# A recurrent kernel's small transfers issued by GpSimd instead of ACT and SP, with a ring of five pieces and 20 of 64 streamed

## The chip, the cores and the metric

The kernel runs on one core of one Trainium2 chip. Its time is device microseconds from start to end of the program on that core; lower is better. All weights and inputs lie in HBM, and the output goes there.

## What is computed

The output is `g * a + (1 - g) * b` for 2048 rows of 1024 numbers, all in bf16. `b` is a feed-forward layer: `gelu(x @ w_gate) * (x @ w_up) @ w_down` with 3584 columns inside. `a` is an attention layer with a memory, which runs over 64 segments of 32 rows one after the other:

```python
g = sigmoid((x * gate_w).sum(-1, keepdims=True))
mem = mem0                                   # 8 rows of 1024
for s in range(64):
    h = concat([mem, x[32*s:32*s+32]])       # 40 rows
    q, k, v = h @ Wq, h @ Wk, h @ Wv         # 32 heads of 128 columns
    p = softmax(masked(q @ k.T * 128**-0.5)) # causal; all rows see the memory
    o = (p @ v) @ Wo                         # 40 rows of 1024
    mem = o[:8]                              # the next segment's memory
    out_a[s] = o[8:]
```

The memory rows make the segments depend on each other: segment s+1 can't start its projections of the memory before segment s has its output rows.

## The kernel before

The program has three stages. A setup (to about 244 us) transposes `x` into a scratch tensor `xq_scr`, computes the gate values, loads the resident weights and computes q, k and v of the last 8 rows of every segment for all segments at once, into the scratch tensors `qk_scr` and `v_scr`. The recurrence (to about 2421 us) runs 64 steps, one for each segment. The last stage is the feed-forward layer, in four blocks of 512 rows, with the mixing of both parts.

**The weights of the recurrence** are Wq, Wk, Wv and Wo, cut into 64 pieces of 128 x 2048 numbers (512 KB, 4 KB in each partition). A step uses the pieces in a fixed order: 8 each of k, q, k, q, v, v (positions 0 to 47), then 16 of Wo (positions 48 to 63). They don't all fit into SBUF: `NRES` of them are resident, and the others are streamed from HBM anew in every step, through a ring of `NRING` buffers. `NRES` is what the memory below the ring leaves: with a ring of 4 it is 45, so 19 of 64 pieces are streamed; the list `streamed` spreads them over the positions by weights. `load_str` (L349) issues the load of the next streamed piece in the order `seq`, on SP's queue, right after the code of the piece that frees a place; the instruction itself waits only for the last readers of its own ring buffer (`ring[n % NRING]`). The setup loads the first pieces, four ahead of their use. A load of 512 KB is one DMA.

**A step** (`for s in range(NSEG)`): `proj(p, s)` is called for the 64 positions in turn, and a table `on(position, function)` puts the rest of the step's work in front of some of them: copies out of PSUM, transposes, scores, softmax, attention. The output is collected in the PSUM bank A0 and copied to `a_bf`; PE transposes it, and DVE copies the 8 memory rows into the `hT` of the next step (L893). That copy closes the step. In this layout a step computes the memory rows and the first 24 rows; the other 8 rows of each segment are collected in `oTR` for four segments, and in every fourth step (s % 4 == 3) Wo is applied to them too: each of its 16 pieces is then used twice, the second time two positions later (`lag`), and the loads that follow on a ring piece are issued after the second use. The result goes to `a_rb`.

**The small transfers of a step**: `load_h` (L488) fetches `hT` of the next step (64 KB) at position 5, `load_qk` (L492) fetches `qkr` (128 KB) at position 33, `load_v` (L496) fetches `vB` (128 KB) for two steps at position 56. `store` (L902, L906) writes `a_bf` (64 KB) into the scratch tensor `a_scr`, and after s % 4 == 3 also `a_rb` in four parts of 16 KB; since these parts overwrite rows that the store of `a_bf` wrote, each waits until that store has landed. `store` is put in a list (`pend`) and issued at position 2 of the next step, behind three of the copies of `put_rest` on POOL. ACT issues `load_h`, `load_qk`, `load_v` and the store of `a_bf`; SP issues the four stores of `a_rb`. The last stage reads `a_scr` long after.

POOL has in a step four copies of `put_rest` (three at position 2, the fourth, `qT` of the second half, at position 30, read by the second `scores` at position 40) and two of `keep_o`.

**Waits.** `_Prog` records every operation with what it reads and writes, and each engine runs its operations in the order of the program, waiting on semaphores for the others. A DMA stands in the queue of the engine that issues it, and its wait holds what is queued behind it. Operations of POOL are chained to each other by a dependency (`self.pool`).

In the text a step is named by its s; "step 0 of each four" is a step with s % 4 == 0.

Of the kernel before, what the change touches and what calls it, by code (L numbers as in the profile page):

```python
# [30 lines left out]
class _Prog:  # L31
# [47 lines left out]
    def op(self, eng, fn, rd=(), wr=(), lane=None, after=()):  # L79
        o = _Op(eng, fn)  # L80
        if lane is not None:
            ln = self.lanes.get(lane)
            if ln is None:
                ln = self.lanes[lane] = [self.new_sem(f"{self.name}_{lane}"), 0, None]
            if ln[2] is not None:
                o.deps.append(ln[2])
            ln[1] += 16
            o.sem, o.val, o.inc, o.need = ln[0], ln[1], 16, True
            ln[2] = o
        for r in rd:  # L90
            self._touch(o, r, False, lane is not None)
        for r in wr:
            self._touch(o, r, True, lane is not None)
        o.deps.extend(after)
        if eng == "pool":
            if self.pool is not None:
                o.deps.append(self.pool)
            self.pool = o
        for d in o.deps:
            d.need = True  # L100
        o.idx = len(self.ops)
        self.ops.append(o)
        return o
# [92 lines left out]
def bass_gated_mix__memory_aug_recurrent_mem_tr__geglu_ffn__prompt_kernel(  # L196
# [16 lines left out]
    S, D = xf.shape  # L213
    _, H, Dh = A_Wq.shape
    M = A_mem0.shape[1]
    SEG = 32
    NR = 24
# [4 lines left out]
    KC = D // 128  # L222
    FF = B_w_gate.shape[1]
    NJ = FF // 128
    NRING = 4
    scale = float(Dh) ** -0.5
    NEG = -1.0e9
    LQ = 40
# [3 lines left out]
    with ExitStack() as es:  # L232
# [10 lines left out]
        xq_scr = nc.dram_tensor("xq_scr", [NT, 128, 4, KC * SEG], BF16)  # L243
        qk_scr = nc.dram_tensor("qk_scr", [128, NSEG, 4, 128], BF16)
        v_scr = nc.dram_tensor("v_scr", [NSEG // 2, 4, 32, 512], BF16)
# [70 lines left out]
        op = P.op  # L316
# [76 lines left out]
        xrT = al("xrT", [128, KC, NRT])  # L393
        stq = [al(f"stq{i}", [128, max(NSEG, 64), 128]) for i in range(2)]
        xq = [al(f"xq{i}", [128, 4, KC, SEG]) for i in range(2)]
        gwb = al("gwb", [128, D])
        assert cur[0] <= top

        tmpv = {p: al(f"tmpv{p}", [128, 2048], at=stq[0].off + PIECE * n) for n, p in enumerate(p for p in str_qkv if p >= 32)}
# [1 line left out]
        vr = [p for p in res if 32 <= p < 48]  # L401
        cur[0] = res[vr[0]].off
        px = [al(f"px{i}", [128, D]) for i in range(min(NT, 16))]
        gp = al("gp", [128, D], FP32, at=xb[0])
        pr = [al(f"pr{i}", [128, D], at=xb[0] + 2048 * i) for i in range(2)]
        memT = al("memT", [128, 64], at=oTR[1].off)
# [78 lines left out]

        def load_h(s):
            t = hT[s % 2]
            op("act", lambda e: e.dma_start(t[:, :, :].rearrange("p k c -> p (k c)"), xq_scr[s // 4, :, s % 4, :]),  # L488
               rd=[("D", "xq", s // 4)], wr=[t.r()], lane=f"h{s % 2}")

        def load_qk(s):
            op("act", lambda e: e.dma_start(qkr[:, :, :], qk_scr[:, s, :, :]), rd=[("D", "qk", m) for m in range(4)],  # L492
               wr=[qkr.r()], lane="qkr")

        def load_v(s):
            op("act", lambda e: e.dma_start(vB[:, :, :].rearrange("p j c -> p (j c)"), v_scr[s // 2].rearrange("g r c -> (g r) c")),  # L496
               rd=[("D", "v", s // SB, g, u) for g in range(4) for u in range(2)], wr=[vB.r()], lane="vb")

        nb2 = [0]
# [336 lines left out]
        for s in range(NSEG):  # L836
# [62 lines left out]
                act_copy(a_rb[:, :], PB[A1][:, 0:256], [BK(A1)], [a_rb.r()])  # L899

            def store(s=s):
                op("act", lambda e: e.dma_start(a_scr[s].rearrange("r (g c) -> g r c", g=4), a_bf[:, :]), rd=[a_bf.r()],  # L902
                   wr=[("D", "a", s)], lane="st")
                if s % 4 == 3:
                    for g in range(4):
                        op("sp", lambda e, g=g: e.dma_start(a_scr[s - 3:s + 1, NR:SEG, 256 * g:256 * g + 256], a_rb[32 * g:32 * g + 32, :]),  # L906
                           rd=[a_rb.r()] + [("D", "a", t) for t in range(s - 3, s + 1)], wr=[("D", "ar", s // 4, g)], lane=f"sr{g}")
            pend.append(store)
        for f in pend:
# [114 lines left out]
```

## Time and profile before

| | |
|---|---|
| median of 3 runs | 3046.32 us (3031.21 to 3049.27) |
| the profiled execution | 3029.77 us, span 3028.0 us |
| busy: PE, DVE, ACT, POOL | 2381.8, 756.8, 627.8, 170.2 us |
| moved by DMA | 805.02 MB |
| mean granted clock of TensorE | 0.930 |

Busy time counts work on the engine; the span is the time from the first to the last instruction. All rows below come from the one profiled execution. In the view of windows, each row has the stretch, its length, the busy time of five engines with instructions in brackets, the granted clock, the mean busy share of the 16 DMA engines and the GB/s that they moved.

### The profile page before, as it was taken

Reading aid. Unit: us, or ns where it says so; the run is one execution under the profiler, and the core shown is the slowest. Engines: PE = TensorE matmul, PEld = TensorE weight load, DVE = VectorE, ACT = ScalarE, POOL = GpSimd, SP = SyncE. Lnnn points to the kernel's source line nnn. Section 1 sums busy time; section 2 is a strip of 40 time slices with the busy share of each in tenths; the row PEclk is TensorE's granted clock in tenths of the full one; section 3 lists DMA queues with packets and bytes.
Section 4 is the critical chain, followed back from the end, with each engine's and each line's share of the span. In section 5 each row is a group of like instructions: output and inputs, shape, how many; then the busy total and the mean of one; then the engine's idle time right before and its main releaser. Section 6 shows DMA issues by size and latency. Waiting matters only on the chain.

```text
span 3028.0 us, 87815 instructions
## 1 busy us (share of the span) xinstructions
PE 2381.8 (79%) x40486; PEld 1104.2 (36%) x40486; DVE 756.8 (25%) x1829; ACT 627.8 (21%) x1461; POOL 170.2 (6%) x487
## 2 busy tenths in 40 slices
PE   7686777777777777777777777777777799999998
PEld 3332333333333333333333333333333344444443
DVE  1311211212121111211121211211121152626262
ACT  1111221222221212212121221222122131313130
POOL 3300000000000000000000000000000000000000
PEclk9798989989999889989898998999899999999999
DMA  8637989989898988989898988989898956060605
GB/s 316 203 120 278 324 294 314 321 297 327 298 330 290 312 296 309 314 290 328 281 323 283 315 305 286 325 299 324 283 324 296 325 213 226 10 229 8 229 8 181
DMA packets 341425, 805.02 MB, mean 266 GB/s; under 512 B 58808, under 2 KB 103864, under 8 KB 341056
## 3 DMA queue, kind: packets, MB, share of 16 engines
q1 hardware_dynamic: 269680, 757.18, 72.3%
q10 hardware_dynamic: 71376, 42.22, 4.6%
q8 instruction: 317, 5.19, 0.7%
q14 instruction: 52, 0.43, 0.0%
HBM read 773.08 MB, written 26.21 MB: 264 GB/s over the span
## 4 chain that ended last, share of the span: by engine, by line
DMA 53%; PE 39%; issue 3%; DVE 2%; SPq 1%; POOL 1%; ACT 1%; ACTq 1%; POOLq 0%
DMA ring<-in_A_Wv_dram 17%; DMA ring<-in_A_Wk_dram 17%; PE pb L941 11%; PE pb L793 10%; DMA ring<-in_A_Wo_dram 7%; DMA ring<-in_A_Wq_dram 7%; PE pb L819 6%; PE pb L978 5%; PE pb L517 2%; DMA a_scr<-a_bf 2%; DMA wd<-in_B_w_down_dram 1%; PE pb L545 1%; POOL gp L475 1%; DMA qk_scr<-stq 1%; PE pb L674 1%
## 5 line engine op out<-in xcount | busy, mean ns | idle before, releaser
L793 PE MATMUL pb<-ring,hT 128*32 128x512 bf16 x3840 | 417.8, 423 | 446.5 <-DMA ring<-in_A_Wk_dram 180.2
L793 PE MATMUL pb<-res,hT 128*32 128x512 bf16 x8448 | 708.7, 417 | 1.1 <-issue 1.1
L793 PEld LDWEIGHTS pb<-ring,hT 128*32 128x32 bf16 x3840 | 106.5, 95 | 623.8 <-DMA ring<-in_A_Wk_dram 215.2
L793 PEld LDWEIGHTS pb<-res,hT 128*32 128x32 bf16 x8448 | 237.4, 102 | 185.4 <-issue 60.0
L657 ACT ACTIVATE tok<-pb 128x512 bf16<-128x512 f32 (+1 forms) x256 | 139.2, 544 | 734.9 <-PE pb L793 729.8
L819 PE MATMUL pb<-res,oT 128*32 128x256 bf16 x6144 | 266.3, 289 | 11.9 <-issue 9.8
L941 PE MATMUL pb<-xT,wg 128*128 128x512 bf16 x896 | 211.8, 379 | 8.4 <-DVE GT L957 8.4
L941 PE MATMUL pb<-xT,wu 128*128 128x512 bf16 x896 | 211.7, 379 | 0.0
L978 PE MATMUL pb<-wd,GT 128*128 128x512 bf16 x896 | 195.5, 379 | 6.7 <-DMA wd<-in_B_w_down_dram 6.7
L819 PEld LDWEIGHTS pb<-res,oT 128*32 128x32 bf16 x6144 | 166.5, 102 | 55.2 <-issue 25.2
L819 PE MATMUL pb<-ring,oT 128*32 128x256 bf16 x2048 | 108.3, 284 | 53.5 <-DMA ring<-in_A_Wo_dram 47.8
L700 DVE TENSOR_REDUCE nm<-pb 128x8 f32<-128x320 f32 x128 | 62.9, 491 | 307.8 <-PE pb L696 307.8
L949 ACT ACTIVATE s<-pb 128x512 f32<-128x512 f32 x112 | 66.8, 596 | 315.1 <-PE pb L941 295.6
L941 PEld LDWEIGHTS pb<-xT,wg 128*128 128x128 bf16 x896 | 86.9, 98 | 116.5 <-DVE GT L957 12.8
L978 PEld LDWEIGHTS pb<-wd,GT 128*128 128x128 bf16 x896 | 87.0, 98 | 114.6 <-DMA wd<-in_B_w_down_dram 11.1
L941 PEld LDWEIGHTS pb<-xT,wu 128*128 128x128 bf16 x896 | 87.7, 98 | 105.7
L517 PE MATMUL pb<-xrT,res 128*128 128x512 bf16 x368 | 101.0, 390 | 29.3 <-DMA ring<-in_A_Wq_dram 29.3
L660 DVE CAST oT<-pb 128x160 bf16<-128x160 f32 x256 | 71.1, 319 | 203.5 <-PE pb L774 203.5
L657 ACT ACTIVATE oT<-pb 128x160 bf16<-128x160 f32 x256 | 63.8, 301 | 270.2 <-PE pb L774 270.2
L660 DVE COPY qT<-pb 128x512 bf16<-128x512 bf16 (+1 forms) x128 | 45.8, 358 | 279.7 <-PE pb L674 187.2
L950 DVE SCALAR_TENSOR_TENSOR tp<-s,pb 128x512 f32<-128x512 f32 x112 | 76.9, 687 | 135.4 <-ACT s L949 135.3
L660 DVE COPY kT<-pb 128x512 bf16<-128x512 bf16 x64 | 27.2, 424 | 329.5 <-PE pb L674 329.5
(101 smaller groups left out, 2278.3 us busy)
## 6 DMA issues: line engine op xcount, KB each, us to landing
ring<-in_A_Wv_dram SPq DMA_DIRECT2D x384, 512.0 KB, 6.2
ring<-in_A_Wq_dram SPq DMA_DIRECT2D x325, 512.0 KB, 6.0
ring<-in_A_Wk_dram SPq DMA_DIRECT2D x260, 512.0 KB, 5.8
ring<-in_A_Wo_dram SPq DMA_DIRECT2D x256, 512.0 KB, 5.8
wd<-in_B_w_down_dram SPq DMA_DIRECT2D x56, 1024.0 KB, 5.8
qk_scr<-stq ACTq DMA_DIRECT2D x4, 2048.0 KB, 12.6
qkr<-qk_scr ACTq DMA_DIRECT2D x64, 128.0 KB, 6.4
res<-in_A_Wk_dram SPq DMA_DIRECT2D x12, 512.0 KB, 11.8
```

What stands on the lines that cost most here:

```text
L475: op("pool", lambda e: e.tensor_tensor(out=gp[:, :], in0=t[:, :], in1=gwb[:, :], op=ALU.mult), rd=[t.r(), gwb.r()], wr=[gp.r()])
L517: ins = e.matmul(PB[b][:, 0:NRT], lhsT=w8[kc][:, c:c + 128], rhs=xrT[:, kc, :], start=(kc == 0), stop=(kc == KC - 1))
L545: ins = e.matmul(PB[bk][0:RB, :], lhsT=xrT[:, kc, RB * b:RB * b + RB], rhs=w8[kc][:, g * 512:g * 512 + 512], start=(kc == 0), stop=(kc == ...
L657: op("act", lambda e: e.activation(o, i, ACTF.Copy), rd=rd, wr=wr)
L660: op("dve", lambda e: e.tensor_copy(o, i), rd=rd, wr=wr)
L700: op("dve", lambda e: e.tensor_reduce(nm[u][:, :, :].rearrange("p a b -> p (a b)"), PB[SS][:, 0:320].rearrange("p (a c) -> p a c", c=LQ), ...
L793: ins = e.matmul(PB[bk][32 * g:32 * g + 32, :], lhsT=h[:, kc, :], rhs=w[:, g * 512:(g + 1) * 512], start=(kc == 0), stop=(kc == KC - 1))
L819: ins = e.matmul(PB[bk][32 * g:32 * g + 32, 0:256], lhsT=o[u][:, gp_, 2 * jj + hh, 0:32], rhs=w[:, c:c + 256], start=(p == 48 and hh == 0) ...
L941: ins = e.matmul(PB[bk][:, 0:FB], lhsT=w[:, kc, cc:cc + 128], rhs=xT[:, :, :, kc, :].rearrange("p t i c -> p (t i) c"), start=(kc == 0), s ...
L949: op("act", lambda e, hg=hg: e.activation(s1[:, :], hg, ACTF.Square, scale=SQ), rd=[BK(bg)], wr=[s1.r()])
L950: op("dve", lambda e, hg=hg, t=t: e.scalar_tensor_tensor(out=t[:, :], in0=s1[:, :], scalar=1.0, in1=hg, op0=ALU.add, op1=ALU.mult), rd=[BK ...
L978: ins = e.matmul(PB[bank[2 * k + hf]][:, :], lhsT=GT[:, j, tb * 128:(tb + 1) * 128], rhs=w[:, jj, hf * 512:(hf + 1) * 512], start=(j == 0) ...
```

## The change

The ring gets five buffers instead of four. The fifth takes the place of one resident piece: 44 pieces are resident and 20 are streamed in a step, at other positions than before. `load_h`, `load_qk`, `load_v` and all stores of `store` are issued by POOL (GpSimd, whose DMAs go through the software queue) instead of ACT and SP. DMAs on POOL are left out of POOL's chain of dependencies. `gwb`, the gate's weights in the setup, lies behind the `px` tiles.

```diff
--- before.py
+++ after.py
@@ -92,7 +92,7 @@
         for r in wr:
             self._touch(o, r, True, lane is not None)
         o.deps.extend(after)
-        if eng == "pool":
+        if eng == "pool" and lane is None:
             if self.pool is not None:
                 o.deps.append(self.pool)
             self.pool = o
@@ -222,7 +222,7 @@
     KC = D // 128
     FF = B_w_gate.shape[1]
     NJ = FF // 128
-    NRING = 4
+    NRING = 5
     scale = float(Dh) ** -0.5
     NEG = -1.0e9
     LQ = 40
@@ -393,7 +393,6 @@
         xrT = al("xrT", [128, KC, NRT])
         stq = [al(f"stq{i}", [128, max(NSEG, 64), 128]) for i in range(2)]
         xq = [al(f"xq{i}", [128, 4, KC, SEG]) for i in range(2)]
-        gwb = al("gwb", [128, D])
         assert cur[0] <= top
 
         tmpv = {p: al(f"tmpv{p}", [128, 2048], at=stq[0].off + PIECE * n) for n, p in enumerate(p for p in str_qkv if p >= 32)}
@@ -401,6 +400,7 @@
         vr = [p for p in res if 32 <= p < 48]
         cur[0] = res[vr[0]].off
         px = [al(f"px{i}", [128, D]) for i in range(min(NT, 16))]
+        gwb = al("gwb", [128, D])
         gp = al("gp", [128, D], FP32, at=xb[0])
         pr = [al(f"pr{i}", [128, D], at=xb[0] + 2048 * i) for i in range(2)]
         memT = al("memT", [128, 64], at=oTR[1].off)
@@ -485,15 +485,15 @@
 
         def load_h(s):
             t = hT[s % 2]
-            op("act", lambda e: e.dma_start(t[:, :, :].rearrange("p k c -> p (k c)"), xq_scr[s // 4, :, s % 4, :]),
+            op("pool", lambda e: e.dma_start(t[:, :, :].rearrange("p k c -> p (k c)"), xq_scr[s // 4, :, s % 4, :]),
                rd=[("D", "xq", s // 4)], wr=[t.r()], lane=f"h{s % 2}")
 
         def load_qk(s):
-            op("act", lambda e: e.dma_start(qkr[:, :, :], qk_scr[:, s, :, :]), rd=[("D", "qk", m) for m in range(4)],
+            op("pool", lambda e: e.dma_start(qkr[:, :, :], qk_scr[:, s, :, :]), rd=[("D", "qk", m) for m in range(4)],
                wr=[qkr.r()], lane="qkr")
 
         def load_v(s):
-            op("act", lambda e: e.dma_start(vB[:, :, :].rearrange("p j c -> p (j c)"), v_scr[s // 2].rearrange("g r c -> (g r) c")),
+            op("pool", lambda e: e.dma_start(vB[:, :, :].rearrange("p j c -> p (j c)"), v_scr[s // 2].rearrange("g r c -> (g r) c")),
                rd=[("D", "v", s // SB, g, u) for g in range(4) for u in range(2)], wr=[vB.r()], lane="vb")
 
         nb2 = [0]
@@ -899,11 +899,11 @@
                 act_copy(a_rb[:, :], PB[A1][:, 0:256], [BK(A1)], [a_rb.r()])
 
             def store(s=s):
-                op("act", lambda e: e.dma_start(a_scr[s].rearrange("r (g c) -> g r c", g=4), a_bf[:, :]), rd=[a_bf.r()],
+                op("pool", lambda e: e.dma_start(a_scr[s].rearrange("r (g c) -> g r c", g=4), a_bf[:, :]), rd=[a_bf.r()],
                    wr=[("D", "a", s)], lane="st")
                 if s % 4 == 3:
                     for g in range(4):
-                        op("sp", lambda e, g=g: e.dma_start(a_scr[s - 3:s + 1, NR:SEG, 256 * g:256 * g + 256], a_rb[32 * g:32 * g + 32, :]),
+                        op("pool", lambda e, g=g: e.dma_start(a_scr[s - 3:s + 1, NR:SEG, 256 * g:256 * g + 256], a_rb[32 * g:32 * g + 32, :]),
                            rd=[a_rb.r()] + [("D", "a", t) for t in range(s - 3, s + 1)], wr=[("D", "ar", s // 4, g)], lane=f"sr{g}")
             pend.append(store)
         for f in pend:
```

## Rows read from the trace of the kernel before

**Rows 1.** The page, part 4: the chain that ended last, shares of the span by engine
```profile
DMA 53%; PE 39%; issue 3%; DVE 2%; SPq 1%; POOL 1%; ACT 1%; ACTq 1%; POOLq 0%
```

**Rows 2.** Groups by line of PE: busy us, mean ns, idle before and its releasers
```profile
L793 PE MATMUL pb<-ring,hT 128*32 128x512 bf16 x3840 | 417.8, 423 | 446.5 <-DMA ring<-in_A_Wk_dram 180.2 <-DMA ring<-in_A_Wv_dram 149.9 <-DMA ring<-in_A_Wq_dram 99.3
```

**Rows 3.** Windows, step 1 of each four (sixteen steps); stretch, length, busy times, clock, DMA, GB/s
```profile
291.17:324.11 32.94, 23.84 (x544) 10.54 (x544) 6.64 (x22) 6.95 (x18) 1.89 (x7) 0.95 0.92 333
...
2320.94:2353.37 32.43, 23.78 (x544) 10.62 (x544) 6.64 (x21) 6.95 (x18) 1.88 (x7) 0.95 0.93 334
sum 512.90, PE 387.56 PEld 173.77 DVE 106.27 ACT 111.05 POOL 30.11; mean PE 24.22 PEld 10.86 DVE 6.64 ACT 6.94 POOL 1.88
```

**Rows 4.** Windows, step 2 of each four (sixteen steps)
```profile
324.11:355.00 30.89, 23.72 (x544) 10.64 (x544) 6.64 (x22) 6.88 (x18) 1.88 (x7) 0.94 0.93 315
...
1130.18:1160.52 30.34, 23.71 (x544) 10.75 (x544) 6.64 (x22) 6.84 (x18) 1.89 (x7) 0.94 0.96 335
...
2353.37:2385.97 32.60, 23.00 (x544) 10.82 (x544) 6.64 (x22) 6.95 (x18) 1.94 (x7) 0.96 0.94 325
sum 505.13, PE 379.04 PEld 174.18 DVE 106.27 ACT 110.75 POOL 30.21; mean PE 23.69 PEld 10.89 DVE 6.64 ACT 6.92 POOL 1.89
```

**Rows 5.** Windows, step 3 of each four (fifteen steps)
```profile
355.00:388.01 33.01, 27.32 (x672) 14.13 (x672) 6.64 (x22) 7.28 (x19) 1.89 (x7) 0.95 0.94 325
...
2250.38:2283.54 33.16, 25.81 (x672) 13.89 (x672) 6.63 (x21) 7.26 (x19) 1.87 (x7) 1.00 0.94 325
sum 524.05, PE 411.94 PEld 215.92 DVE 99.62 ACT 108.68 POOL 28.33; mean PE 27.46 PEld 14.39 DVE 6.64 ACT 7.25 POOL 1.89
```

**Rows 6.** Windows, step 0 of each four, from step 4 on (fifteen steps)
```profile
388.01:426.34 38.33, 26.42 (x544) 11.31 (x544) 6.63 (x22) 7.01 (x19) 1.89 (x7) 0.82 0.79 265
...
2283.54:2320.94 37.40, 25.44 (x544) 10.79 (x544) 6.64 (x22) 7.01 (x19) 1.89 (x7) 0.86 0.80 267
sum 552.72, PE 380.78 PEld 165.89 DVE 99.58 ACT 104.93 POOL 28.16; mean PE 25.39 PEld 11.06 DVE 6.64 ACT 7.00 POOL 1.88
```

**Rows 7.** Waits of the SP queue: waiter, releaser, us in total, times, longest
```profile
SPq L906 <- DMA a_scr<-a_bf: 72.7, 16, 5.8
```

**Rows 8.** Timeline of the SP queue, start of step 28: start us, length us
```profile
1195.02 0.33 SPq L349 DMA_DIRECT2D ring<-in_A_Wk_dram  x1
1199.45 2.47 SPq L906 DMA_DIRECT2D a_scr<-a_rb  x4
1201.96 0.45 SPq L349 DMA_DIRECT2D ring<-in_A_Wk_dram  x1
```

**Rows 9.** Windows of 3 us within that hold
```profile
1199.00:1202.00 3.00, 1.82 (x32) 0.67 (x32) 0.23 (x1) 0.60 (x1) 0.00 (x0) 1.00 0.23 84
1202.00:1205.00 3.00, 0.93 (x16) 0.33 (x8) 0.42 (x1) 0.00 (x0) 0.00 (x0) 1.00 0.58 167
```

**Rows 10.** Timeline of PE, the same step
```profile
1206.10 0.62 PE L793 MATMUL pb<-ring,hT 128*32 128x512 bf16 x4 [3.17 <-DMA ring<-in_A_Wk_dram]
```

**Rows 11.** Windows, 3 us at the end of step 27
```profile
1190.00:1193.00 3.00, 2.98 (x112) 2.92 (x116) 0.00 (x0) 0.00 (x0) 0.00 (x0) 1.00 0.53 172
```

**Rows 12.** DMA issues: KB each, median us from issue to landing
```profile
q10 hardware_dynamic: 71376, 42.22, 4.6%
...
qkr<-qk_scr ACTq DMA_DIRECT2D x64, 128.0 KB, 6.4
```

**Rows 13.** Timeline of the ACT queue, start of step 28
```profile
1194.12 0.51 ACTq L902 DMA_DIRECT2D a_scr<-a_bf  x1
```

**Rows 14.** Timeline of POOL, start of step 29
```profile
1231.60 0.29 POOL L826 COPY kT<-qkr 128x128 bf16<-128x128 bf16 x1
1242.47 0.42 POOL L826 COPY qT<-qkr 128x128 bf16<-128x128 bf16 x1 [10.58 <-PE pb L720]
```

**Rows 15.** Timeline of PE, second scores of step 29
```profile
1250.33 0.38 PE L696 MATMUL pb<-kT,qT 128*32 128x40 bf16 x32
```

**Rows 16.** Groups by line of POOL, its longest operation
```profile
L475 POOL TENSOR_TENSOR gp<-px,gwb 128x1024 f32<-128x1024 bf16 x16 | 33.9, 2121 | 60.9 <-DVE dl L477 60.7 <-POOL mR L364 0.2
```

## The prediction

> **What bounds the kernel now.** I read the chain that ended last first: 53% of it is DMA against 39% PE [rows 1], and what PE waits for in the recurrence is streamed pieces: 446.5 us of idle time before the projections from the ring [rows 2]. Then I cut the recurrence at the DVE copies that close each step (the one that writes the memory rows of the next `hT`) and asked for windows by kind of step. The reader should compare length and DMA share. Steps 1 and 2 of each four take 512.90/16 = 32.06 and 505.13/16 = 31.57 us [rows 3, 4], step 3 takes 524.05/15 = 34.94 [rows 5], step 0 takes 552.72/15 = 36.85 [rows 6]: 135.4 us a round. The means of the DMA share in these 62 rows are 0.941, 0.941, 0.898 and 0.813, so the DMA engines are idle for 1.89, 1.86, 3.56 and 6.89 us in a step of each kind, 14.2 us a round, and carry for the other 121.2 us. A plain step is bound by the stream: PE is busy 24.2 and 23.7 us of it [rows 3, 4].
>
> Why step 0 is longer, though it computes what step 1 does, shows in SyncE's queue [rows 7, 8]. The stores of `a_rb` wait there until the store of `a_bf` (issued by ACT) has landed: 72.7 us over 16 times. In step 28 a ring load goes out at 1195.02, nothing until 1199.45, four stores of 2.47 us together, and the next ring load at 1201.96. The DMA engines fall to shares of 0.23 and 0.58 [rows 9], and PE then waits 3.17 us for a piece [rows 10]. Step 3 idles for another reason: its second output projection makes PE run 16 pieces twice, and while PE is at it (2.98 us of 3.00 busy) the ring is full and the share is 0.53 [rows 11].
>
> The accounting I use is: length of a round = time the DMA engines carry + time they idle. It fits because PE (24.2 + 23.7 + 27.5 + 25.4 = 100.8 us a round) stays below both parts together.
>
> **Part by part.**
>
> *The stores of `a_rb` leave SP.* The `a_rb` stores and their wait go to POOL. What SP loses is the hold, 4.5 us of waiting and 2.47 us of issue. The price is that step 0 becomes a plain one: 36.85 - 31.82 = 5.03 us, and by the other view its DMA idle time falls from 6.89 to 1.87, 5.02 us. There are 15 such steps, 4 to 60 (the sixteenth hold stands behind the last step and delays nothing that PE waits for in the recurrence): 15 x 5.02 = 75 us. From below, the bare PE wait of 3.17 us gives 48; from above 6.89 x 15 = 103. What is late next is the stream itself.
>
> The Trainium skill, "DMA: Bandwidth & Descriptors", section "Issuing engines are not separate DMA queues", says that issuing from several engines only saves the sequencer time of the issue. By that rule 15 x 2.47 = 37 us come back here (rival 3); the rows above show a wait of 72.7 us beside the issue, which the rule does not count, and I go by them.
>
> *One piece more per step is streamed.* By the same windows [rows 3, 4] the 32 plain steps move 326 GB/s in the mean at a share of 0.941, so the engines carry 326/0.941 = 347 GB/s while they carry, and a piece (128 x 2048 in bf16, 512 KB) is 0.524 MB / 347 GB/s = 1.51 us. 64 x 1.51 = +97 us. Nothing hides it while the stream is the bound: that is its upper bound; the lower is 0, if the idle time took it up, and that is counted in the next item.
>
> *The ring gets a fifth slot.* A load waits for the readers of its own slot, so SP can have five pieces out where it had four. No row shows a ring of five. It gives nothing at worst; at best it ends all idle time that is left: 1.87 x 47 + 3.56 x 16 = 145 us. In plain steps the idle time is made of short gaps, and a further piece of 1.51 us in hand covers about half: 0.87 each, 47 x 0.87 = 41 us (a choice, nearer to the middle than to an end). In step 3 it is one long gap, and a further piece shortens it by its own time: 16 x 1.51 = 24 us. Together -65.
>
> *Three loads and the a_bf store leave ACT for GpSimd's software queue.* ACT issues of this kind take 0.51 us [rows 13], ACT is 1% of the chain [rows 1], and its work waits for PE; I take 0, with 30 us (that 1%) as the most to gain. The bytes stay. Whether software-made transfers cost the 16 engines more is not shown. All small transfers of the ACT queue had 4.6% of 16 engines' time for 42.22 MB [rows 12], 139 us, and by the sizes in the code half of these bytes move in the recurrence: 70 us. Taken at 0 (same bytes, same runs); twice as dear would be +70, half as dear -35. Latency is covered: `qkr` is asked for about half a step before its copies, and landed in 6.4 us [rows 12]; `hT` and `vB` a whole step to most of one ahead.
>
> *What is queued on POOL.* In a step 0 the order becomes three copies of `put_rest`, the a_bf store, the wait for its landing (5.3 us from its issue [rows 8, 13]), four stores, the load of `hT`, then the fourth copy, into `qT`, whose reader is the second scores. In step 29, a plain one, POOL is free from 1231.89, its fourth copy starts at 1242.47 [rows 14], and the scores that read it at 1250.33 [rows 15]: 18.0 us of cover without the copy. 5.3 us of wait and six issues fit if an issue takes under (18.0 - 5.3)/6 = 2.1 us. ACT's took 0.51 [rows 13]; POOL's own longest operation took 2.12 [rows 16]. I take about 1 us, nearer to the issue of the same transfer, hence 0. From both ends, 0 to 15 x 6 x 0.02 = 2 us.
>
> *Setup and the last stage.* One resident piece less is loaded ahead of the first step; the gate row `gwb` lies behind the `px` tiles and only delays a late v piece's load by what already delays its neighbours; `load_h(0)` and its like follow POOL's setup work. 0 for all; the feed-forward stage keeps its loads.
>
> *Sum:* -75 + 97 - 65 = -43 us. The profiled execution took 3029.77 us (span 3028.0), 0.5% below the median of the three runs, 3046.32; the change brings it to about 2987, and the median to about **3003 us**.
>
> **Rivals.**
>
> 1. *The fifth slot gives nothing* (or is never filled: the setup hands out only four loads ahead of use, and the program might keep to that). Then -75 + 97 = +22, 3068 us. For it: the share is 0.94 already in plain steps. Against: a plain step did run at 0.96 and 335 GB/s in 30.34 us [rows 4], and SP's order holds no wait but that for the slot, so it does run five ahead.
> 2. *The idle time nearly all goes:* -75 + 97 - 145 = -123, 2923 us. Against: step 3's gap is longer than a piece.
> 3. *Only the issue time comes back*, because the ring's four pieces hide SP's wait: -37 + 97 - 65 = -5, 3041 us. Against: the shares of 0.23 and 0.58 in the hold [rows 9].
> 4. *GpSimd becomes late* (the slower side). Place: the fourth POOL copy in step 0, behind six software issues and a landing. It decides from 2.1 us per issue; at 3 us the second scores start 6 x 0.9 = 5.4 us late, 15 times: +81, and -43 + 81 = +38, so 3084 us. For it: POOL works in order, and POOL's compute operations reach 2.12 us. Against: PE's wait there lets the ring fill, which gives part back. The Trainium skill, "DMA: Bandwidth & Descriptors", section "SWDGE vs HWDGE vs iDMA", says that GpSimd writes such descriptors into SBUF and that DVE can lock it out of there in some of its modes; no row here shows a software issue, so the trace neither agrees nor contradicts.
>
> **How the numbers follow.** The forecast (-20 to -75) has 0.48, of which 0.34 lies beyond 30 us. Rival 2 and what lies towards it has 0.13, rival 1 0.20 and its form "never filled" 0.03, rival 3 0.04, rival 4 0.12. One per cent, 30 us, is about what a measurement of this kernel tells from no change. Faster: 0.34 + 0.13 = 0.47. Slower: 0.11 of rival 4 and 0.06 of rival 1 with dearer small transfers = 0.17. Same: 0.36. The range runs from 2940, most of the way to rival 2, to 3080, close to rival 4.
>
> **What would show it.** SP's wait on `a_scr` is gone and no DMA window in a step 0 falls to 0.2; step 0 lasts 32 to 33 us, steps 1 and 2 about 32.5 (31.8 + 1.5 - 0.9), step 3 about 35; DMA share in plain steps 0.96 or more. Steps 1 and 2 at 33.3 would say rival 1. PE waiting for POOL in the second scores would say rival 4. What would make the number wrong above all is the worth of the fifth slot, the one term that no row shows.

## The result, and the profile after

The changed kernel takes 2883.53 us (median of 4 runs, 2874.0 to 2895.46) against 3047.8 (4 runs): a ratio of 0.9474, 95% interval 0.9424 to 0.9523. That is 160 us or 5.3% faster, and below the range that was predicted (2940 to 3080, forecast 3003). The profiled execution took 2882.88 us, span 2881.1.

The page of the changed kernel: the DMA queues (packets, MB, share of 16 engines' span; SP issues on q1, ACT on q10, POOL on q0), and the chain that ended last.

```profile
q1 hardware_dynamic: 284512, 789.16, 76.3%
q0 software_dynamic: 13824, 22.16, 2.4%
q10 hardware_dynamic: 39888, 21.24, 2.4%
...
DMA 47%; PE 43%; issue 4%; DVE 2%; ACT 1%; POOL 1%; ACTq 1%; SPq 0%; POOLq 0%
```

SP's queue now moves 789.16 MB where it moved 757.18: the twentieth piece. Yet DMA's part of the chain falls from 53% [rows 1] to 47%. The small transfers of the step have gone from q10 to q0, and all small transfers together cost the engines what they cost before: 2.4% and 2.4% of 2881 us are 138 us, where q10 had 4.6% of 3028, 139 us [rows 12]. (q0 now has the `a_rb` stores too, which were on q1; alone on q0, in run 1 below, they have 0.1%.)

PE's group of projections from the ring waits 286.1 us where it waited 446.5 [rows 2]:

```profile
L793 PE MATMUL pb<-ring,hT 128*32 128x512 bf16 x3840 | 403.1, 409 | 286.1 <-DMA ring<-in_A_Wk_dram 103.7 <-DMA ring<-in_A_Wv_dram 83.6 <-DMA ring<-in_A_Wq_dram 70.3
```

The windows by kind of step, steps 1, 2, 3 and 0 of each four (first step of the kind and the sum over 16, 16, 15 and 15 steps; length, busy times, clock, DMA share, GB/s), answer to [rows 3 to 6]:

```profile
291.36:320.69 29.33, 23.35 (x544) 10.40 (x544) 6.66 (x22) 6.96 (x18) 4.16 (x12) 1.00 1.03 388
...
sum 491.63, PE 388.06 PEld 174.55 DVE 106.33 ACT 110.63 POOL 66.79; mean PE 24.25 PEld 10.91 DVE 6.65 ACT 6.91 POOL 4.17
...
320.69:350.20 29.51, 23.11 (x544) 10.71 (x544) 6.64 (x22) 6.85 (x18) 3.63 (x11) 0.94 1.00 353
...
sum 485.82, PE 383.66 PEld 172.16 DVE 106.33 ACT 110.35 POOL 57.94; mean PE 23.98 PEld 10.76 DVE 6.65 ACT 6.90 POOL 3.62
...
350.20:381.70 31.50, 26.11 (x672) 13.82 (x672) 6.65 (x21) 7.18 (x19) 4.16 (x11) 1.00 0.98 355
...
sum 509.74, PE 414.00 PEld 218.08 DVE 99.68 ACT 108.02 POOL 63.59; mean PE 27.60 PEld 14.54 DVE 6.65 ACT 7.20 POOL 4.24
...
381.70:412.07 30.37, 23.21 (x544) 10.41 (x544) 6.65 (x22) 7.02 (x19) 6.05 (x15) 1.00 1.01 372
...
sum 459.87, PE 347.62 PEld 157.80 DVE 99.70 ACT 105.15 POOL 89.43; mean PE 23.17 PEld 10.52 DVE 6.65 ACT 7.01 POOL 5.96
```

The steps last 30.73, 30.36, 33.98 and 30.66 us where they lasted 32.06, 31.57, 34.94 and 36.85. Two things are to be seen. Step 0 is a plain step now, as forecast. But steps 1 and 2, which were to get longer by half a microsecond, got 1.3 and 1.2 us shorter with a piece more to load: the DMA share is 0.986 in the mean, and the 16 engines move 355 GB/s in a plain step where they moved 326.

SP's queue at the start of a step 0 of the changed kernel (s = 28, start us, length us): ring loads go on throughout.

```profile
1138.00 1.35 SPq L349 DMA_DIRECT2D ring<-in_A_Wk_dram  x2
1139.46 4.84 SPq L349 DMA_DIRECT2D ring<-in_A_Wq_dram  x4
1145.84 6.48 SPq L349 DMA_DIRECT2D ring<-in_A_Wv_dram  x4
```

POOL at the same place: the a_bf store, then the wait for its landing, four a_rb stores, the load of `hT`, and the copy into `qT`.

```profile
1138.33 0.72 POOL L902 DMA_DIRECT2D a_scr<-a_bf  x1
1145.89 2.35 POOL L906 DMA_DIRECT2D a_scr<-a_rb  x4 [6.83 <-issue]
1148.23 0.59 POOL L488 DMA_DIRECT2D hT<-xq_scr  x1
1151.53 0.41 POOL L826 COPY qT<-qkr 128x128 bf16<-128x128 bf16 x1 [2.71 <-PE pb L720]
```

It is POOL that waits now, 6.8 us here. This row names no releaser; over the whole run eleven of these waits, 63.6 us, are put down to the landing of the a_bf store, for which the program makes them wait. POOL's issues take about 0.6 to 0.7 us, and the `qT` copy still waits 2.71 us for PE (L720) before it starts; in all fifteen steps 0 from step 4 on it waits 0.8 to 6.2 us for PE. So POOL isn't late.

### The profile page after: what moved, and what is told of

Same layout as the page of the kernel before. It is cut to its first block, busy times and chain, and to the rows that moved or that the text cites. A ratio compares the mean times of both kernels' runs of the same rounds, so it can differ in the third digit from the quotient of the medians.

```text
span 2881.1 us, 88022 instructions
## 1 busy us (share of the span) xinstructions
PE 2355.2 (82%) x40448; PEld 1097.0 (38%) x40486; DVE 757.5 (26%) x1829; ACT 627.0 (22%) x1461; POOL 337.8 (12%) x775
## 3 DMA queue, kind: packets, MB, share of 16 engines
q1 hardware_dynamic: 284512, 789.16, 76.3%
q0 software_dynamic: 13824, 22.16, 2.4%
q10 hardware_dynamic: 39888, 21.24, 2.4%
## 4 chain that ended last, share of the span: by engine, by line
DMA 47%; PE 43%; issue 4%; DVE 2%; ACT 1%; POOL 1%; ACTq 1%; SPq 0%; POOLq 0%
DMA ring<-in_A_Wq_dram 17%; DMA ring<-in_A_Wv_dram 13%; PE pb L941 11%; PE pb L793 11%; PE pb L819 8%; DMA ring<-in_A_Wk_dram 7%; DMA ring<-in_A_Wo_dram 6%; PE pb L978 6%; PE pb L517 2%; DMA wd<-in_B_w_down_dram 1%; PE pb L545 1%; PE pb L674 1%; POOL gp L475 1%; DMA qk_scr<-stq 1%; ACTq L472 1%
## 5 line engine op out<-in xcount | busy, mean ns | idle before, releaser
L793 PE MATMUL pb<-res,hT 128*32 128x512 bf16 x8448 | 671.2, 404 | 2.0 <-issue 2.0
L793 PE MATMUL pb<-ring,hT 128*32 128x512 bf16 x3840 | 403.1, 409 | 286.1 <-DMA ring<-in_A_Wk_dram 103.7
L793 PEld LDWEIGHTS pb<-res,hT 128*32 128x32 bf16 x8448 | 215.6, 100 | 165.6 <-issue 43.2
L819 PE MATMUL pb<-res,oT 128*32 128x256 bf16 x5632 | 247.7, 281 | 37.7 <-issue 37.4
L819 PE MATMUL pb<-ring,oT 128*32 128x256 bf16 x2560 | 140.9, 283 | 54.0 <-DMA ring<-in_A_Wo_dram 24.6
L819 PEld LDWEIGHTS pb<-res,oT 128*32 128x32 bf16 x5632 | 150.8, 99 | 60.0 <-issue 49.0
L831 POOL COPY oTR<-oT 128x128 bf16<-128x128 bf16 x128 | 37.6, 294 | 828.3 <-DVE oT L660 828.3
L826 POOL COPY qT<-qkr 128x128 bf16<-128x128 bf16 x128 | 45.0, 351 | 587.6 <-PE pb L720 582.5
L819 PEld LDWEIGHTS pb<-ring,oT 128*32 128x32 bf16 x2560 | 61.4, 97 | 119.9 <-issue 56.3
```

The lines of the kernel that those rows point to most:

```text
L793: ins = e.matmul(PB[bk][32 * g:32 * g + 32, :], lhsT=h[:, kc, :], rhs=w[:, g * 512:(g + 1) * 512], start=(kc == 0), stop=(kc == KC - 1))
L819: ins = e.matmul(PB[bk][32 * g:32 * g + 32, 0:256], lhsT=o[u][:, gp_, 2 * jj + hh, 0:32], rhs=w[:, c:c + 256], start=(p == 48 and hh == 0) ...
L826: op("pool", lambda e: e.tensor_copy(t[:, :, :, 32:40].rearrange("p j g c -> p (j g) c"), qkr[:, m, :].rearrange("p (x c) -> p x c", c=8)) ...
L831: op("pool", lambda e: e.tensor_copy(oTR[u][:, :, :, 8 * i:8 * i + 8].rearrange("p g j c -> p (g j) c"), oT[u][:, :, :, 32:40].rearrange(" ...
```

## The experiments

A cause for the shorter plain steps had to be found. **Theory D** said that the deeper ring makes the stream faster and the end of SP's hold gives the rest. **Theory Q** said that the stream is faster because the small transfers have left the hardware's queues. Ratios are to the kernel before on the same chip, with 95% intervals; microseconds are the ratio's distance from 1 times 3046. All runs keep two small parts of the change, `gwb` behind the `px` tiles and DMAs outside POOL's chain; no run tests these by themselves. A plain step is a step 1 or 2 of each four. The landing of a load is the time from its issue until the trace reports it as landed.

**1. The a_rb stores alone.** Everything else as before:

```diff
-    op("sp",   lambda e, g=g: e.dma_start(a_scr[s - 3:s + 1, NR:SEG, ...], a_rb[...]),
+    op("pool", lambda e, g=g: e.dma_start(a_scr[s - 3:s + 1, NR:SEG, ...], a_rb[...]),
```

> The kernel before with one part of the change: the four stores of a_rb are issued by POOL, the ring stays at 4 with 19 pieces streamed, loads and the a_bf store stay on ACT. Theory D (the hold of SP is worth 75 us, the deeper ring the rest): steps 0 of each four fall from 36.85 to about 32 us, 3048 - 75 = 2973 us, steps 1 and 2 stay at 31.6 to 32.1. Theory Q (what makes the stream faster is that all small transfers leave the queues that the hardware generates): the same 2973. Rival, only the issue time of the four stores comes back: 3048 - 37 = 3011.

2964.89 us, ratio 0.9728 (0.9687 to 0.9769): -83 us. Step 0 of each four (first and sum over 15 steps):

```profile
390.08:420.91 30.83, 23.21 (x544) 10.51 (x544) 6.62 (x21) 7.01 (x19) 4.36 (x11) 1.00 0.95 324
...
sum 470.72, PE 352.89 PEld 162.46 DVE 99.56 ACT 104.73 POOL 63.28; mean PE 23.53 PEld 10.83 DVE 6.64 ACT 6.98 POOL 4.22
```

That is 31.38 us a step, no longer than a plain step of this run (32.23). The 15 steps 0 together are 82 us shorter than before (36.85 - 31.38 = 5.47 us each), so the gain lies where [rows 3 to 6] put it (75 us forecast).

**2. The ring alone.** The changed kernel with all small transfers put back: 44 pieces resident and 20 streamed, the loads and the a_bf store on ACT, the a_rb stores on SP. Against the kernel before:

```diff
-    NRING = 4
+    NRING = 5
```

> The changed kernel with all small transfers back on ACT and SP: ring of 5 with 20 streamed, nothing else. Theory D: steps 1 and 2 at about 30.5 us as in the changed kernel (packets of the ring faster, share 0.98), steps 0 still held by SP for about 5 us, so 2884 + 75 = about 2960 us. Theory Q: the fifth slot gives nothing or my 65 us, the twentieth piece costs 97: 3080 to 3145 us, steps 1 and 2 at 32.5 to 33.3.

2943.31 us, ratio 0.9661 (0.9597 to 0.9726): -103 us, against a forecast of +32 for these two terms (+97 - 65). Steps 2 and steps 0:

```profile
320.00:348.52 28.52, 24.19 (x544) 11.21 (x544) 6.64 (x21) 6.92 (x18) 1.83 (x6) 0.89 1.00 366
...
sum 466.79, PE 374.10 PEld 169.14 DVE 106.24 ACT 110.39 POOL 30.25; mean PE 23.38 PEld 10.57 DVE 6.64 ACT 6.90 POOL 1.89
...
383.62:421.70 38.08, 24.37 (x544) 10.55 (x544) 6.64 (x21) 7.02 (x19) 1.88 (x7) 0.91 0.84 298
...
sum 547.55, PE 369.21 PEld 165.21 DVE 99.61 ACT 104.57 POOL 28.29; mean PE 24.61 PEld 11.01 DVE 6.64 ACT 6.97 POOL 1.89
```

Step 2 takes 466.79/16 = 29.2 us, less than in the changed kernel (30.4), and the engines' share is 1.0 in the mean. Step 0 takes 36.5: the hold costs 7 us in this kernel, for SP's wait has got longer, 87.9 us in all where it was 72.7 [rows 7]:

```profile
SPq L906 <- DMA a_scr<-a_bf: 87.9, 16, 7.0
```

**3. The queue alone.** All small transfers of the step on POOL, ring of 4, 19 streamed. Against the changed kernel:

```diff
-    NRING = 5
+    NRING = 4
```

> The kernel before with all small transfers on POOL, ring of 4 and 19 streamed. Theory D: no more than the end of the hold, about 2973 us, steps 1 and 2 at 31.6 to 32.1. Theory Q: the stream runs as fast as in the changed kernel with one piece less, steps 1 and 2 at 29 to 29.5 us, below 2850 us.

2975.44 us, ratio 0.976 (0.9717 to 0.9803): -73 us, no better than the a_rb stores alone. Steps 1:

```profile
294.95:325.54 30.59, 22.53 (x544) 10.41 (x544) 6.64 (x21) 6.85 (x18) 4.16 (x11) 1.00 0.96 341
...
sum 509.71, PE 376.90 PEld 171.25 DVE 106.21 ACT 110.34 POOL 66.64; mean PE 23.56 PEld 10.70 DVE 6.64 ACT 6.90 POOL 4.16
```

These steps take 31.86 us, where they took 32.06; all plain steps take 32.2, where they took 31.8. Theory Q falls.

**4. The piece alone.** The kernel before, with 20 pieces through a ring of 4:

```diff
-    NRES = (top - cur[0]) // PIECE
+    NRES = 64 - 20
```

> The kernel before with 20 pieces streamed through the ring of 4 (the fifth place lies unused), small transfers on ACT and SP. Prices the piece: at the full 1.51 us in each step +97, 3145 us, steps 1 and 2 at 33.3. If the packets get cheaper or idle time takes part of it, less: +50, 3098. Below zero only if the other choice of positions matters more than the piece.

3197.95 us, ratio 1.0495 (1.0435 to 1.0556): +151 us, more than the +97 that a piece costs at the engines' rate. Steps 1:

```profile
296.80:328.53 31.73, 23.20 (x544) 10.33 (x544) 6.63 (x22) 6.95 (x18) 1.88 (x7) 1.00 0.92 318
...
sum 555.80, PE 417.31 PEld 181.71 DVE 106.16 ACT 110.41 POOL 30.13; mean PE 26.08 PEld 11.36 DVE 6.63 ACT 6.90 POOL 1.88
```

These steps take 34.74 us, 2.7 more than before, though the share fell to 0.91 in the mean of the sixteen. A piece that takes 1.51 us of the engines at 347 GB/s cost 2.7 us. So it isn't that rate alone that prices a piece in a ring of four. The twenty streamed positions are other ones than the nineteen; no run separates them from the piece.

**Theory L** takes that up: a place (a buffer) of the ring goes round in landing + waiting for PE + the next issue, and a step of n pieces through k places lasts n/k such rounds, however much the engines could carry. (This round of a place is not the round of four steps that the prediction adds up.) As long as the landing doesn't grow in proportion with the places, a place more shortens the step.

**5. The changed kernel with a ring of 4,** small transfers on POOL:

```diff
-    NRING = 5
+    NRING = 4
-    NRES = (top - cur[0]) // PIECE
+    NRES = 64 - 20
```

> The changed kernel with a ring of 4, still 20 streamed (the fifth place unused). Theory L (each place of the ring goes round in landing plus some 0.8 us, so a step lasts pieces x round / places until the engines' ceiling): steps 1 and 2 at 20 x 6.9 / 4 = 34.5 us as in the run of the piece alone, less the hold: 3198 - 90 = about 3110 us. Theory of the prediction (carried bytes plus short gaps, fifth place worth 65 us): 2884 + 65 = 2949 us.

3132.57 us, ratio 1.0304 (1.027 to 1.0339). Steps 1 and the landing of a ring load (min, median, max):

```profile
294.04:329.23 35.19, 26.01 (x544) 11.05 (x544) 6.64 (x21) 6.96 (x18) 4.18 (x11) 0.90 0.92 313
...
sum 551.46, PE 407.81 PEld 177.00 DVE 106.22 ACT 110.89 POOL 66.95; mean PE 25.49 PEld 11.06 DVE 6.64 ACT 6.93 POOL 4.18
```

```profile
DMA to landing us min/median/max: 3.6/6.1/15.0
```

These steps take 34.47 us (34.5 expected by theory L). Here the streamed positions are those of the change, and only the place is missing. So the fifth place is worth (1.0304 - 0.9474) x 3046 = 253 us in the changed kernel, and from runs 2 and 4, (1.0495 - 0.9661) x 3046 = 254 without POOL: the forecast said 65, its upper bound 145. Against run 3, the piece with its positions costs (1.0304 - 0.976) x 3046 = 166 us here.

**6. Ring of 5, only the a_rb stores on POOL.** Against the changed kernel:

```diff
-    op("pool", ... in load_h, load_qk, load_v and the store of a_bf
+    op("act",  ...
```

> The changed kernel with the loads and the a_bf store back on ACT; only the stores of a_rb are issued by POOL. Theory D (ring and end of the hold are all of the gain, the software queue for the other transfers costs a little): steps 0 fall from the 36.5 us of the run with the ring alone to about 29.7 as steps 1 and 2 there, 2943 - 15 x 6.8 = about 2841 us, faster than the change's 2884. If the software queue itself helps the stream: not below 2884.

2855.19 us, ratio 0.9407 (0.9389 to 0.9424); 2841 were expected. It is faster than the change (0.9474, 0.9424 to 0.9523) by (0.9474 - 0.9407) x 3046, some 20 us, the intervals just touching. Steps 1:

```profile
sum 481.38, PE 377.96 PEld 172.03 DVE 106.19 ACT 110.08 POOL 30.00; mean PE 23.62 PEld 10.75 DVE 6.64 ACT 6.88 POOL 1.87
```

They take 30.09 us, where the change has 30.73.

**7. The loads back on ACT, all stores on POOL.** Against the changed kernel:

```diff
-    op("pool", ... in load_h, load_qk, load_v
+    op("act",  ...
```

> The changed kernel with the three loads back on ACT; all stores on POOL. If the software loads are what costs a microsecond in steps 1 and 2 (30.1 and 29.2 with the ring alone, 30.7 and 30.4 with the change): as the run with only the a_rb stores on POOL, about 2841 us. If it is the a_bf store: about 2884.

2874.17 us (2854.47 to 2892.96), ratio 0.9463 (0.9447 to 0.9479): nearer to the change than to run 6. That speaks for the a_bf store as the part that costs in the software queue, but the spread of these five executions, 38 us, is wider than the 19 us to run 6, and why it should cost wasn't found.

**8. Ring of 6, 21 streamed, a_rb on POOL, the rest on ACT.** Against run 6:

```diff
-    NRING = 5
+    NRING = 6
```

> Ring of 6 with 21 streamed, a_rb stores on POOL, the other small transfers on ACT. If five places have brought the engines to their ceiling in the plain steps, the sixth piece of memory costs 1.45 us a step (+93) and only the step with the second output projection gains (at most 16 x 1.5 = 24): about 2910 us, slower than the ring of 5. If places still bind: below 2841.

2819.53 us, ratio 0.9284 (0.9263 to 0.9305): faster than both kernels and than run 6. The branch of the expectation in which five places had brought the engines to their ceiling, 2910 us, is out. Steps 1 and the landing:

```profile
267.56:299.47 31.91, 24.41 (x544) 10.77 (x544) 6.64 (x21) 6.85 (x18) 1.96 (x7) 0.95 1.03 387
...
sum 472.31, PE 378.73 PEld 172.46 DVE 106.22 ACT 110.17 POOL 30.43; mean PE 23.67 PEld 10.78 DVE 6.64 ACT 6.89 POOL 1.90
```

```profile
DMA to landing us min/median/max: 3.7/7.6/15.9
```

That is 29.5 us a step and a share of 1.02 for 21 pieces. Of the 38 us between the two profiled executions (spans 2852.2 and 2813.7; the medians differ by 36) about 24 lie ahead of the end of step 0 (267.56 us instead of 291.38 at the first of the closing copies); why that part got shorter is open. The recurrence behind it gains 16 us (1903.7 against 1920.2 from the first of these copies to the last), and only these speak for the place.

**9. Ring of 3, 19 streamed, a_rb on POOL.** Here the theories stand furthest apart. Against run 1:

```diff
-    NRING = 4
+    NRING = 3
-    NRES = (top - cur[0]) // PIECE
+    NRES = 64 - 19
```

> Ring of 3 with 19 streamed (the fourth place unused), a_rb stores on POOL, the rest on ACT. Theory L: a place goes round in landing (about 5.5 us with three out) plus 0.8, so a plain step lasts 19 x 6.3 / 3 = 40 us, about 3460 us in all. Theory of the prediction (bytes carried at a fixed price plus gaps): 2965 and about 65 to 97 more, 3030 to 3060.

3423.44 us, ratio 1.1252 (1.1217 to 1.1287). Steps 1 and the landing:

```profile
304.12:342.41 38.29, 26.59 (x544) 11.58 (x544) 6.64 (x22) 6.85 (x18) 1.93 (x7) 0.83 0.81 269
...
sum 623.81, PE 432.92 PEld 185.89 DVE 106.20 ACT 110.84 POOL 30.33; mean PE 27.06 PEld 11.62 DVE 6.64 ACT 6.93 POOL 1.90
```

```profile
DMA to landing us min/median/max: 3.5/5.4/14.6
```

These steps take 39.0 us, with the engines busy 0.82 of the time: close to theory L's 40, and not the 33 to 34 of the accounting by carried bytes. The whole takes 3423 us, where theory L said 3460 and the accounting 3030 to 3060.

**10. Ring of 7, 22 streamed.** The last line moves the place where the last stage's tiles begin (its list of free memory follows). Against run 8:

```diff
-    NRING = 6
+    NRING = 7
-    extra = {..., 26: 4, ..., 40: 4, ...}
+    extra = {..., 26: 3, ..., 40: 3, ...}
-    cur[0] = res0
+    cur[0] = res0 - PIECE
```

> Ring of 7 with 22 streamed, a_rb stores on POOL, the rest on ACT (the weights that spread the streamed pieces changed a little, and the last stage's tiles begin one place lower, so that both fit). If the engines are at their ceiling of some 386 GB/s with six places: 11.87 MB a step in 30.8 us, a microsecond more than with six, about 2870 us. If places still pay: at most 2820.

2869.42 us, ratio 0.9429 (0.9391 to 0.9466): slower than six. Steps 1 and the landing:

```profile
289.26:322.93 33.67, 24.98 (x544) 10.91 (x544) 6.63 (x21) 6.95 (x18) 1.93 (x7) 0.93 1.03 400
...
sum 485.89, PE 388.52 PEld 176.69 DVE 106.17 ACT 111.11 POOL 30.14; mean PE 24.28 PEld 11.04 DVE 6.64 ACT 6.94 POOL 1.88
```

```profile
DMA to landing us min/median/max: 3.7/8.8/16.3
```

These steps take 30.4 us at 393 GB/s in the mean, where run 8 had 29.5 at 386. The landing has grown from 7.6 to 8.8 us, nearly in proportion with the places, and the place no longer pays for the piece that it takes. Of the 66 us between the profiled executions of runs 8 and 10, though, 22 lie ahead of the end of step 0 (289.26 us instead of 267.56); the recurrence loses 41, some 0.7 us a step. The positions changed a little too, and no run separates that.

**11. The stores late instead of elsewhere.** The four stores leave `store`, which is called at position 2 of the next step, for a function at position 20, still on SP. The kernel before, nothing on POOL:

```diff
-                if s % 4 == 3:
-                    for g in range(4):
-                        op("sp", ... a_rb ...)
+            on(20, store_late)
```

> The kernel before (ring of 4, 19 streamed, no transfer issued by POOL), with the four stores of a_rb issued by SP at position 20 of the next step instead of position 2, when the a_bf store has landed. If the wait was what cost, and not the queue: as with POOL, 2965 to 2975 us, steps 0 at 31.5 to 32. If the 2.47 us of issue on SP cost too: some 20 us more, 2990. If the hold of SP was not the cause of the long steps 0: 3040.

2975.07 us, ratio 0.9771 (0.9744 to 0.9798): -70 us of the -83 that POOL gives, the intervals overlapping. SP's wait is nearly gone, with the four stores still in SP's queue (L914 is their line here). Steps 0 take 492.96/15 = 32.9 us, more than the 31.5 to 32 expected and than run 1's 31.38; the stores' issue on SP may be in that, which no run separates.

```profile
SPq L914 <- DMA a_scr<-a_bf: 5.7, 4, 2.1
```

```profile
sum 492.96, PE 361.25 PEld 164.29 DVE 99.57 ACT 105.24 POOL 28.19; mean PE 24.08 PEld 10.95 DVE 6.64 ACT 7.02 POOL 1.88
```

**12. The same with a ring of 6.** Against run 11:

```diff
-    NRING = 4
+    NRING = 6
```

> Ring of 6 with 21 streamed, no transfer issued by POOL: a_rb stores on SP at position 20, the rest on ACT. If GpSimd's queue has no part in the gain but to take the wait off SP: 2820 us, as the ring of 6 with a_rb on POOL. If SP's issue of four stores costs the deeper ring as well: up to 2850.

2839.37 us, ratio 0.9323 (0.9292 to 0.9354), 12 us slower than run 8 ((0.9323 - 0.9284) x 3046, the intervals just overlapping). The wait is back, 54.8 us where the ring of 4 had 5.7, and step 0 takes 484.92/15 = 32.3 us:

```profile
SPq L914 <- DMA a_scr<-a_bf: 54.8, 14, 5.6
```

```profile
355.80:390.73 34.93, 27.36 (x544) 11.74 (x544) 6.64 (x21) 7.01 (x19) 1.88 (x7) 0.80 0.93 326
...
sum 484.92, PE 366.17 PEld 163.81 DVE 99.59 ACT 104.85 POOL 28.32; mean PE 24.41 PEld 10.92 DVE 6.64 ACT 6.99 POOL 1.89
```

SP issues as soon as a place is free, so with six places it comes to the stores earlier, before the a_bf store has landed: its last ring issue ahead of the stores ends 5.1 us after the issue of the a_bf store in the mean of these steps, with four places 8.3 us. Position 20 of the program isn't a time.

## Why the prediction was wrong, step by step

**The hold of SP: right.** -75 forecast, -83 measured by itself (run 1). That most of it is the wait and not the issue is shown by run 11, where 70 us come back although SP still issues the four stores. The Trainium skill, "DMA: Bandwidth & Descriptors", section "Issuing engines are not separate DMA queues", says that issuing from several engines saves only the time of the issue, which would be 37 us here (rival 3). The runs measured 83 and 70, and the measurement decides. The same section of the Trainium skill says that the transfers of all issuers run on the same 16 engines. Run 3 agrees: moving them to another queue by itself made plain steps no faster (32.2 us against 31.8).

**The piece and the fifth place: the step that failed.** The prediction put +97 - 65 = +32; runs 6 and 1 measure (0.9407 - 0.9728) x 3046 = -98 for both together, once the hold is gone, and the change against run 3, which differs from it in nothing else, (0.9474 - 0.976) x 3046 = -87. At a ring of four the piece cost 151 or 166 (runs 4 and 5), where 97 was its upper bound, and the fifth place gave 253 or 254, where 145 was. The step that failed is the accounting "length of a round = time the DMA engines carry + time they idle", used with a fixed price for what is carried (121.2 us, and 1.51 for each further piece) and with a fifth place that takes from the idle time only. Runs 3 and 5 and the change show both parts. The other three kinds of step of run 3, in the order 2, 3, 0, and then of run 5:

```profile
sum 519.88, PE 389.90 PEld 174.99 DVE 106.21 ACT 110.69 POOL 58.42; mean PE 24.37 PEld 10.94 DVE 6.64 ACT 6.92 POOL 3.65
sum 527.80, PE 417.25 PEld 219.06 DVE 99.55 ACT 108.47 POOL 62.28; mean PE 27.82 PEld 14.60 DVE 6.64 ACT 7.23 POOL 4.15
sum 476.02, PE 355.27 PEld 163.72 DVE 99.60 ACT 104.88 POOL 90.64; mean PE 23.68 PEld 10.91 DVE 6.64 ACT 6.99 POOL 6.04
sum 551.07, PE 415.95 PEld 178.39 DVE 106.19 ACT 110.60 POOL 58.26; mean PE 26.00 PEld 11.15 DVE 6.64 ACT 6.91 POOL 3.64
sum 560.15, PE 438.09 PEld 219.95 DVE 99.58 ACT 108.48 POOL 64.46; mean PE 29.21 PEld 14.66 DVE 6.64 ACT 7.23 POOL 4.30
sum 529.31, PE 386.42 PEld 164.81 DVE 99.58 ACT 105.04 POOL 89.11; mean PE 25.76 PEld 10.99 DVE 6.64 ACT 7.00 POOL 5.94
```

With the mean DMA share of each kind of step, four steps come to:

| us in four steps | run 3: 4 places, 19 pieces | run 5: 4 places, 20 pieces | the change: 5 places, 20 pieces |
|---|---|---|---|
| length | 131.3 | 141.5 | 125.7 |
| carried (length x share) | 120.6 | 128.2 | 122.2 |
| idle | 10.7 | 13.3 | 3.6 |

From run 3 to the change the carried time rose by 1.6 us where 4 x 1.51 = 6.0 was forecast, and the idle time fell by 7.1 where 65/16 = 4.1 was. Over 16 rounds of four steps these are 71 and 49 us, together about the 119 between +32 and -87. The fifth place alone (run 5 to the change) took 9.7 us of idle time and 6.1 us of carried time out of four steps, 16 x 15.8 = 253 us; the second part is what the prediction held fixed.

So the busy share of the DMA engines isn't work at a fixed price; it also passes 1 (1.02 in run 8), so that 1 less the share is only roughly idle time. Over the whole run q1 moved 757.18 MB in a share of 72.3% of 3028 us before, 346 GB/s while busy:

```profile
q1 hardware_dynamic: 269680, 757.18, 72.3%
```

After, by the page above, it is 789.16 MB in 76.3% of 2881.1 us, 359 GB/s; with places from 3 to 7 it goes 331, 347, 363, 372, 378 (runs 9, 1, 6, 8, 10, from the same rows of their pages). Why the engines carry the same bytes in less time with more places is not shown by any run. The rows of before gave a hint: the 347 GB/s that I took for the engines' rate was a mean over plain steps, and single windows of 3 us ran above it, with PE still waiting for pieces:

```profile
1163.00:1166.00 3.00, 2.21 (x40) 0.86 (x36) 0.22 (x1) 0.60 (x1) 0.00 (x0) 1.00 1.02 367
```

What was left out is the loop of a place. The rows were in the trace of before; the landing of its ring loads is

```profile
DMA to landing us min/median/max: 3.5/5.9/15.0
```

and a plain step of 31.81 us [rows 3, 4] through 4 places for 19 pieces gives a round of 31.81 x 4/19 = 6.70 us, that is the landing plus 0.8. In the changed kernel

```profile
DMA to landing us min/median/max: 3.5/6.7/15.9
```

and 30.55 x 5/20 = 7.64 us. Over the runs (plain step: mean of the 32 steps 1 and 2; landing: median of all ring loads; round: step x places / pieces):

| run | places, pieces | plain step us | round us | landing us | round less landing |
|---|---|---|---|---|---|
| 9 | 3, 19 | 38.73 | 6.1 | 5.4 | 0.7 |
| 1 | 4, 19 | 32.23 | 6.8 | 5.9 | 0.9 |
| 5 | 4, 20 | 34.45 | 6.9 | 6.1 | 0.8 |
| the change | 5, 20 | 30.55 | 7.6 | 6.7 | 0.9 |
| 6 | 5, 20 | 30.09 | 7.5 | 6.6 | 0.9 |
| 8 | 6, 21 | 29.62 | 8.5 | 7.6 | 0.9 |
| 10 | 7, 22 | 30.42 | 9.7 | 8.8 | 0.9 |

That all places go round n/k times a step is how a round is defined; what is measured is that the landing fills it but for the last column, which hardly moves, and that the landing grows more slowly than the number of places. Followed load by load in the traces (loads issued in plain steps, means), the time from one issue into a place to the next is 6.68 us before, 7.66 in the change and 9.63 in run 10, and from the landing to that next issue 0.71, 0.91 and 1.14 us: PE's use of a piece and SP's next issue are a small part of the round in all of them. From three to five places the landing grows by 1.2 us, 22%, while the places grow by 67%, so each place buys time. From six to seven it grows by 16% with 17% more places, and next to nothing is left to buy. A DMA share of 0.94 made a kernel that was bound by its round look like one that was bound by bandwidth. A fixed round isn't the whole price of a piece either: with the 6.70 us of before, 20 pieces through 4 places would last 33.5 us, and runs 4 and 5 measure 34.8 and 34.5, because the round itself grew to 7.0 and 6.9.

**Small transfers by the software queue: taken at 0, measured +20 us** with a ring of 5 (the change against run 6), and +10 with a ring of 4 ((0.976 - 0.9728) x 3046, inside the intervals). The bounds of -35 and +70 held. The engines' time for them didn't change, so the cost is elsewhere. It lies in the plain steps (30.55 us against 30.09) and in step 3 (33.98 against 33.36) and hardly in step 0, where POOL waits (30.66 against 30.47); why the stream is slower there wasn't found.

**Setup and last stage: taken at 0, and so they came out.** The first closing copy comes at 291.36 us, before at 291.17.

**The sum by runs:** -83 (hold), -98 (piece and place) and +20 (software queue) stand where the prediction had -75, +32 and 0. That they add up to the -160 of the change proves nothing, since each is the difference to the run before it.

**The rivals.** Rival 1 (the fifth slot gives nothing) and its form "never filled" are excluded by run 5, and the change has 4.4 ring loads out in the mean of its plain steps where the kernel before had 3.6. Rival 2, the idle time nearly all gone (2923 us), came nearest: the share did reach 0.986; but its price, 145 us, was the bound that the failed step set. Rival 3 falls by runs 1 and 11. Rival 4's place was right and its price not paid: issues on POOL take 0.59 to 0.72 us, under the 2.1 from which it decides.

## What to carry to other kernels

For a stream through a ring, work out the round of a place first: step x places / pieces, beside the landing. If they nearly agree, each piece costs at least a round divided by the places (6.70/4 = 1.7 us here; 151/64 = 2.4 were measured, as the round grew with it), and one buffer more can be worth more than the piece of memory that it takes; it stops paying when the landing grows as fast as the places. A busy share of the DMA engines near 0.94 is no proof that they are the bound: look for windows that ran faster, and test with a buffer less, which here moved more than a buffer more. And a store that waits for another store's landing belongs on a queue that nothing urgent stands behind; putting it later in the program helps only as long as the queue doesn't run ahead to it.

## What the runs showed of the hardware that was not expected

The time that the engines are busy for a given number of bytes falls when more loads of 512 KB are out: 331 GB/s while busy with a ring of three, 346 and 347 with four, 378 with seven, where 2.6, 3.6 and 6.2 ring loads are out in the mean of the plain steps. POOL's issue of a small transfer took 0.59 to 0.72 us in the timeline above, ACT's 0.51 for the a_bf store [rows 13]. The software queue moved its 22.16 MB in 13824 packets, 1.6 KB each in the mean. The hardware queues had used 33792 for the same transfers, 71376 - 39888 on q10 and 2304 on q1 (269680 before, 267376 in run 1), 0.65 KB each, at the same engine time as far as the shares tell.
